# A recurrence, a mixture of experts and a squared-relu MLP on one core: token numbers copied to a tile of their own, the MLP in two passes over halves of its inner dimension, half of the weight conversions moved under the first pass

## The chip, the cores and the metric

The kernel runs on one core of a Trainium2 chip. The metric is device time in microseconds (us) of that core, as the median of several runs. The core's engines are TensorE (PE in the profile, its weight loads PEld), VectorE (DVE), ScalarE (ACT), GpSimd (POOL) and SyncE (SP), which here issues most of the DMAs. Each engine works through its own instructions in order and waits for others by semaphores.

## The reference

Three layers follow each other. All inputs are drawn at random; the MLP's weights `w_in` and `w_out` reach the kernel as float64 words.

```python
# 1. recurrence: batch 4, heads 8, seq 768, head_dim 48
for t in range(S):
    cur = np.einsum('bhd,bhe->bhde', u[None] * kt, vt)
    y[:, :, t] = np.einsum('bhd,bhde->bhe', rt, state + cur)
    state = wt[:, :, :, None] * state + np.einsum('bhd,bhe->bhde', kt, vt)
# 2. x: 3072 tokens x 384; 8 experts of width 1024, each token goes to one
e_idx = np.argmax(x @ w_gate, axis=1)
...
for e in range(E):
    h = np.maximum(x[mask] @ w1[e], 0.0)
    out[mask] = gate_w[mask, None] * eom[mask, e, None] * (h @ w2[e])
# 3. MLP: 384 -> 2048 -> 384
r = np.maximum(x @ w_in, 0.0)
out = (r * r) @ w_out
```

## The kernel before

The work runs in three stages. The recurrence (and the routing of its tokens) takes the first 285 us and is not touched.

**Experts.** The tokens of each expert form a block; blocks 1 to 7 hold room for 480, 440, 416, 404, 396, 388 and 384 tokens (`CAPS`). A block's rows are gathered from DRAM by POOL (`gather`, four indirect DMAs into `xg`, of which there is one buffer), scaled by their gate on ACT (`scale`), transposed on PE (`prep_x`, three per block) and split into a high and a low float32r part. Every product is made of three matmuls of such parts (`three`). The inner dimension of 1024 is walked in `KF` = 8 steps: `up(f)` is nine matmuls into `ph`, `down(f)` nine into the accumulators `po`. The weights arrive by SP's DMAs in halves (`load`) and are split three steps ahead: the high parts on ACT, the low part `w1l` on POOL, `w2l` on DVE. While block e is multiplied, block e+1 is loaded (f = 1 and 5), gathered (f = 2), scaled (f = 4) and transposed (f = 5, 6, 7). `put_ids`, issued by SP at f = 7, writes the numbers of the block's tokens from the last column of `xg` to DRAM (`x2_ids`, one 4-byte value to a row); `put` writes its results to `x2_cols`, one column to a token.

**Conversions.** Under blocks 1 to 7 the MLP's weights are turned from float64 to float32 on DVE: 32 pieces of 128x384, each in two steps, `convert_1` (three DVE instructions) and `convert_2` (three on DVE and a sum on POOL), loaded to `cq` and stored as `wi_f` and `wo_f`. `convert_step` does one step at a time, nine or ten per block.

**MLP.** The 3072 tokens form `NG` = 6 groups of 512. For each group the `KF2` = 16 steps of the inner dimension follow each other: `up2` is nine matmuls of 512 columns into `ph`, then relu on ACT (`rl`), square on DVE (`gg`), high part on ACT (`gh`), low part on DVE (`gl`); `down2` is twelve matmuls of 384 columns into four accumulators, three called `po` (one buffer each) and one `px`. PE's order is up2(n), down2(n-1), up2(n+1). After a group's last step the accumulators are copied to `ob`, by ACT and DVE in turn, and POOL writes them to the output by an indirect DMA.

The order on PE, DVE, ACT and SP is that of the code (`tc.manual_schedule`); POOL is in the scheduler's own order.

Of the kernel before, what the change touches and what calls it, by code (L numbers as in the profile page):

```python
# [21 lines left out]
def rwkv_moe_kernel(  # L22
# [64 lines left out]
    # of each expert: tokens, where its rows of each batch are, and from which of its tokens on  # L87
# [6 lines left out]
    # of each block  # L94
# [65 lines left out]
    def route_steps(b, xT, xr, wk, ps_t, ordered=False):  # L160
# [69 lines left out]
        if b == B - 2:  # L230
# [5 lines left out]
            # where its tiles' results go; a tile without a token goes past all  # L236
# [16 lines left out]
    def rows_of(gt, bv, K, nb):  # L253
        # where a block's rows come from; a slot past its tokens reads the row of zeros
# [12 lines left out]
    def finish_routing():  # L267
        # expert 0 first, the others by the number of their tokens
# [16 lines left out]
        # the first tokens of expert 0 have a block of their own  # L285
# [37 lines left out]
    with ExitStack() as actx:  # L323
# [230 lines left out]
    class Block:  # L554
        def __init__(self, P, cap, w1e, w2e, gcol):
# [3 lines left out]
            # where accumulators and transposes go  # L559
# [18 lines left out]
        def scale(self, eng=None):  # L578
            # the gate is not negative, so that it may come before the relu
# [61 lines left out]
        def put_ids(self, at):  # L641
            i, n = divmod(self.cap, 128)
            if i:
                nc.sync.dma_start(x2_ids[ds(at, i * 128)].rearrange("(i p) o -> p (i o)", p=128), self.xg[:, :i, DM + 1])
            if n:
                nc.sync.dma_start(x2_ids[i * 128:][ds(at, n)], self.xg[:n, i, DM + 1:DM + 2])
# [4 lines left out]
        # few tokens: they stand still, the weights stream  # L651
# [31 lines left out]
        def again(self, upto):  # L683
            # a block's first steps anew, into the same tiles; the sums begun there are closed first
# [10 lines left out]
        def whole(self, at):  # L695
# [3 lines left out]
            self.gather()  # L699
            self.put_ids(at)  # L700
            self.scale()
# [465 lines left out]
```

## Time and profile before

| | us |
|---|---|
| median of the runs | 979.07 |
| runs | 978.92, 979.07, 2810.91 |
| span of the profiled execution | 978.1 |

No own time is listed for the profiled execution beside its span. The span goes from its first to its last instruction and lies 0.97 us under the median of the runs.

| engine | busy us | share of the span |
|---|---|---|
| PE | 893.6 | 91% |
| PEld | 767.4 | 78% |
| DVE | 556.0 | 57% |
| ACT | 356.7 | 36% |
| POOL | 343.0 | 35% |

The shares are means over three stages with different limits; in the page's 40 slices PE falls to 6 to 8 tenths between slice 13 and slice 23 and is full after that, while DVE is at 6 to 9 tenths in the same slices and at 3 behind them. A stage is read from its own windows and waits.

### The profile page before, as it was taken

The page shows a single profiled execution, that of the slowest core. Times are in us where ns is not written, and L with a number is a line of the kernel's source. Part 1 is how long each engine was busy: PE and PEld are TensorE (multiplying, and loading weights), DVE is VectorE, ACT ScalarE, POOL GpSimd, SP SyncE. Part 2 cuts the span into 40 slices and gives each one's busy share as a digit, 9 for nine tenths or more (in the row PEclk, how much of TensorE's full clock was granted, in tenths as well). Part 3 has the DMA queues.
Part 4 walks back from the last instruction along what each step waited for, and adds up shares of the span by engine and source line. Part 5 has one row for each costly group of instructions (what it writes and reads, how often), then busy time and mean ns, then how long its engine had stood idle before and what let it go on. Part 6 is the DMA issues. An engine that isn't in the chain of part 4 may idle for free.

```text
span 978.1 us, 14225 instructions
## 1 busy us (share of the span) xinstructions
PE 893.6 (91%) x5324; PEld 767.4 (78%) x5324; DVE 556.0 (57%) x959; ACT 356.7 (36%) x721; POOL 343.0 (35%) x339
## 2 busy tenths in 40 slices
PE   4999999999786669898798899999999999999995
PEld 3667676777675559787698899999989999889995
DVE  6678887666824658677799733333333333333332
ACT  4235544233223234343344445432323323323221
POOL 9436564523411534435544744310201201101101
PEclk8589999999789799897999999999999999999998
DMA  9735463401134657757568634200200200000000
GB/s 197 206 75 111 97 147 74 110 2 64 48 107 110 210 125 232 193 168 245 186 189 231 187 91 129 82 33 1 65 1 0 65 1 1 33 1 1 33 1 33
DMA packets 152657, 94.99 MB, mean 97 GB/s; under 512 B 111996, under 2 KB 138540, under 8 KB 152580
## 3 DMA queue, kind: packets, MB, share of 16 engines
q1 hardware_dynamic: 146692, 79.12, 30.7%
q0 software_dynamic: 4912, 14.65, 4.3%
q8 instruction: 44, 0.72, 0.3%
q10 hardware_dynamic: 976, 0.22, 0.1%
q14 instruction: 33, 0.27, 0.1%
HBM read 73.05 MB, written 20.92 MB: 96 GB/s over the span
## 4 chain that ended last, share of the span: by engine, by line
issue 27%; PE 20%; DMA 9%; DVE 8%; POOL 5%; ACT 1%; SPq 1%; POOLq 0%; DVEq 0%; ACTq 0%
DMA x_ids<-xg 6%; PE ph L542 3%; PE ph L540 3%; PE ph L541 3%; PE po L541 3%; PE po L542 3%; PE po L540 3%; DVE cbf L923 2%; POOL out_dram L982 2%; DMA wo_f<-caf 1%; POOL xg L575 1%; DVE w2l L535 1%; DVE cq L921 1%; DVE hl L532 1%; DVE caf L920 1%
## 5 line engine op out<-in xcount | busy, mean ns | idle before, releaser
L966 DVE SCALAR_TENSOR_TENSOR gg<-ph,rl 128x512 f32<-128x512 f32 x96 | 66.4, 692 | 190.7 <-ACT rl L964 190.7
L964 ACT ACTIVATE rl<-ph 128x512 f32<-128x512 f32 x96 | 57.5, 599 | 186.4 <-PE ph L542 186.3
L535 DVE TENSOR_TENSOR gl<-gg,gh 128x512 fp32r<-128x512 f32 x96 | 66.7, 695 | 65.9 <-PE px L542 49.4
L531 ACT ACTIVATE hh<-ph 128x320 fp32r<-128x320 f32 (+7 forms) x64 | 32.5, 508 | 184.2 <-PE ph L542 180.5
L534 ACT CAST gh<-gg 128x512 fp32r<-128x512 f32 x96 | 59.5, 620 | 72.7 <-DVE gg L966 72.7
L535 POOL TENSOR_TENSOR w1l<-w1r,w1h 128x384 fp32r<-128x384 f32 x56 | 60.6, 1087 | 62.4 <-ACT w1h L534 62.3
L541 PE MATMUL po<-hl,w2h 128*128 128x320 f32 (+7 forms) x192 | 69.8, 364 | 11.8 <-DVE hl L532 11.7
L540 PE MATMUL po<-hh,w2h 128*128 128x320 f32 (+7 forms) x192 | 70.1, 372 | 1.9 <-DVE yT L637 1.9
L542 PE MATMUL po<-hh,w2l 128*128 128x320 f32 (+7 forms) x192 | 68.3, 356 | 0.0
L535 DVE TENSOR_TENSOR w2l<-w2r,w2h 128x384 fp32r<-128x384 f32 x64 | 54.4, 857 | 8.9 <-ACT w2h L534 8.3
L982 POOL DMA_INDIRECT out_dram<-ob,tokc x24 | 24.9, 1038 | 98.1 <-ACT ob L980 92.6
L535 POOL TENSOR_TENSOR x20l<-x2r,x20h 128x512 fp32r<-128x512 f32 x6 | 7.8, 1293 | 146.9 <-ACT x20h L534 146.9
L542 PE MATMUL ph<-x0h,w1l 128*128 128x320 f32 (+7 forms) x64 | 24.7, 386 | 32.8 <-POOL w1l L535 32.8
L532 DVE SCALAR_TENSOR_TENSOR hl<-ph,hh 128x320 fp32r<-128x320 f32 (+7 forms) x64 | 36.6, 572 | 26.8 <-ACT hh L531 26.7
L575 POOL DMA_INDIRECT xg<-x_rows,gi x28 | 27.3, 974 | 69.8 <-DMA x_ids<-xg 45.5
L541 PEld LDWEIGHTS po<-hl,w2h 128*128 128x128 f32 x192 | 37.9, 197 | 17.5 <-DVE hl L532 16.4
L456 PE MATMUL pa<-rA,kT 64*128 64x128 f32 x384 | 48.2, 316 | 2.3 <-DVE A L458 2.3
L477 PE MATMUL py<-A,vN 128*64 128x128 f32 x384 | 48.4, 310 | 0.0
L481 PE MATMUL py<-rA,St 64*64 64x128 f32 x320 | 47.8, 330 | 0.0
L456 PEld LDWEIGHTS pa<-rA,kT 64*128 64x128 f32 x384 | 37.4, 206 | 11.6 <-issue 6.5
L924 POOL TENSOR_TENSOR caf<-caf,cbf 128x384 f32<-128x384 f32 x32 | 33.3, 1041 | 33.0 <-DVE cbf L923 33.0
L438 POOL TENSOR_SCALAR_AFFINE_SELECT A<-g 128x1536 f32<-128x1536 f32 x16 | 30.7, 1921 | 38.4 <-DVE g L436 20.2
(796 smaller groups left out, 2564.4 us busy)
## 6 DMA issues: line engine op xcount, KB each, us to landing
w1r<-in_moe_w_dram SPq DMA_DIRECT2D x16, 768.0 KB, 5.4
w2r<-in_moe_w_dram SPq DMA_DIRECT2D x16, 768.0 KB, 6.9
cq<-in_moe_w_in_dram SPq DMA_DIRECT2D x16, 384.0 KB, 5.2
cq<-in_moe_w_out_dram SPq DMA_DIRECT2D x16, 384.0 KB, 5.6
wD<-in_w_dram SPq DMA_DIRECT2D x32, 144.0 KB, 3.0
kN<-in_k_dram SPq DMA_DIRECT2D x32, 144.0 KB, 3.0
rN<-in_r_dram SPq DMA_DIRECT2D x32, 144.0 KB, 3.1
vN<-in_v_dram SPq DMA_DIRECT2D x32, 144.0 KB, 2.7
```

The source lines that it names most:

```text
L456: nc.tensor.matmul(pa[j][:, ci], kT[pp, hf * HC + ci], rAb[pp, hf * HC + ci], start=True, stop=True)
L477: nc.tensor.matmul(py[64 * j:64 * j + 64, ci], vN[:, c, j], A[:, c, j], start=True, stop=c == 0)
L481: nc.tensor.matmul(py[pp, ci], St[pp, :, c], rAb[pp, c], start=False, stop=True)
L532: nc.vector.scalar_tensor_tensor(lo, src, 0.0, hi.bitcast(F32), op0=ALU.max, op1=ALU.subtract)
L534: nc.scalar.copy(hi, src)
L535: lo_eng.tensor_tensor(lo, src, hi.bitcast(F32), op=ALU.subtract)
L540: nc.tensor.matmul(out_, a_of(ah), b_of(bh), start=start, stop=False)
L541: nc.tensor.matmul(out_, a_of(ah), b_of(bl), start=False, stop=False)
L542: nc.tensor.matmul(out_, a_of(al), b_of(bh), start=False, stop=stop)
L964: nc.scalar.activation(rl, ph, AF.Relu)
L966: nc.vector.scalar_tensor_tensor(gg, ph, 0.0, rl, op0=ALU.max, op1=ALU.mult)
L982: ins = nc.gpsimd.indirect_dma_start(out=out[:, :], out_offset=IndirectOffsetOnAxis(ap=tokc[:, n:n + 1], axis=0), in_=ob, in_offset=None)
```

## The change

Three things are changed together; some comment lines go as well.

First, `scale` copies the token numbers from `xg` to a tile `xid` (three buffers), and `put_ids` reads that copy. Block 0 has no `scale` and keeps its `xg`.

Second, the MLP runs in two passes. The first takes steps f = 0 to 7 of all six groups and stores each group's sums to a DRAM tile `part`; the second takes f = 8 to 15, loads the parts and adds them on DVE as the sums leave PSUM. The tokens are loaded and split in both passes; `ob` has three buffers where it had six, and the next group is loaded at the first step of a group (it was the eighth of sixteen) and split at its steps 2, 4 and 6 (they were 10, 12 and 14).

Third, only the pieces of f = 0 to 7 are converted under the experts, in five steps per block. The other 16 pieces are loaded and converted in steps 8 to 39 of the MLP's first pass, one `convert_1` or `convert_2` to a step, and split straight from the converted tile without the way through DRAM.

```diff
         def scale(self, eng=None):
+            if self.ids is None:
+                self.ids = self.P.xb.tile([128, NTL], F32, name="xid", bufs=3)
+            i, n = divmod(self.cap, 128)
+            for ids, num in ([(self.ids[:, :i], self.xg[:, :i, DM + 1])] if i else []) + \
+                            ([(self.ids[:n, i:i + 1], self.xg[:n, i, DM + 1:DM + 2])] if n else []):
+                if eng:
+                    eng.tensor_copy(ids, num)
+                else:
+                    nc.scalar.copy(ids, num)
...
         def put_ids(self, at):
             i, n = divmod(self.cap, 128)
+            ids = self.xg[:, :, DM + 1] if self.ids is None else self.ids
             if i:
-                nc.sync.dma_start(x2_ids[ds(at, i * 128)].rearrange("(i p) o -> p (i o)", p=128), self.xg[:, :i, DM + 1])
+                nc.sync.dma_start(x2_ids[ds(at, i * 128)].rearrange("(i p) o -> p (i o)", p=128), ids[:, :i])
...
+    FH = KF2 // 2
+    part = [dram.tile([128, DM], F32, name=f"part{n}") for n in range(NT // 128)]
...
+    def split_converted(n):
+        f, which = divmod(n, 2)
+        (wi, wo)[which][f] = split([wp.tile([128, DM], F32R, name=f"w{'io'[which]}{f}{q}") for q in "hl"], converted.pop(n), nc.gpsimd)
...
+    def load_part(s):
+        for i in range(NI):
+            n = (s - NG) * NI + i
+            parts[n] = pbp.tile([128, DM], F32, name="pp")
+            nc.sync.dma_start(parts[n], part[n])
...
-            if f == KF2 - 1:
+            if l == FH - 1:
                 ob = obp.tile([128, DM], F32, name="ob")
-                if i % 2:
-                    nc.vector.tensor_copy(ob, pos[g][i][:, :DM])
-                else:
-                    nc.scalar.copy(ob, pos[g][i][:, :DM])
-                n = g * NI + i
+                n = s % NG * NI + i
+                if fs == 0:
+                    if i % 2:
+                        nc.vector.tensor_copy(ob, pos[s][i][:, :DM])
+                    else:
+                        nc.scalar.copy(ob, pos[s][i][:, :DM])
+                    nc.sync.dma_start(part[n], ob)
+                    continue
+                nc.vector.tensor_tensor(ob, pos[s][i][:, :DM], parts.pop(n), op=ALU.add)
...
-    NCV = 2 * KF2
-    steps2 = [(g, f) for g in range(NG) for f in range(KF2)]
+    NCV = 2 * FH
+    steps2 = [(s, f) for s in range(2 * NG) for f in range(s // NG * FH, s // NG * FH + FH)]
...
-            convert_step()
-            if f in (2, 7):
+            if f % 2 == 0 or f == KF - 1:
                 convert_step()
...
-        for n, (g, f) in enumerate(steps2):
+        late = [(fn, n) for n in range(NCV, 2 * KF2) for fn in (convert_1, convert_2)]
+        convert_load(NCV)
+        convert_load(NCV + 1)
+        for n, (s, f) in enumerate(steps2):
+            l = f % FH
             if n > 1:
-                up2(gb, g, f)
+                up2(gb, s, f)
...
-            if f == 7 and g + 1 < NG:
-                load_x(g + 1)
-            if g + 1 < NG and f in (10, 12, 14):
-                prep_x2(xb3 if g % 2 == 0 else xb2, g + 1, f // 2 - 5)
+            if l == 0 and s + 1 < 2 * NG:
+                load_x(s + 1)
+            if s >= NG and l == 3:
+                load_part(s)
+            if s + 1 < 2 * NG and l in (2, 4, 6):
+                prep_x2(xb3 if s % 2 == 0 else xb2, s + 1, l // 2 - 1)
+            if s and late:
+                fn, m = late.pop(0)
+                fn(m)
+                if fn is convert_1:
+                    if m + 2 < 2 * KF2:
+                        convert_load(m + 2)
+                    if m > NCV:
+                        split_converted(m - 1)
+                elif not late:
+                    split_converted(m)
             if n and n < len(steps2) - 2:
                 down2(*steps2[n - 1])
```

On POOL, under block 1, this stood before: the splits of block 1's first three steps, then the gather of block 2 (four indirect DMAs), then splits again, and `caf`, the sum that ends a conversion.

```order
L535 TENSOR_TENSOR w1l<-w1r,w1h 128x3x128 x3
L575 DMA xg<-x_rows,gi 128x386 x3
L575 DMA xg<-x_rows,gi 56x386
L535 TENSOR_TENSOR w1l<-w1r,w1h 128x3x128 x2
L924 TENSOR_TENSOR caf<-caf,cbf 128x384
```

And this stands there now:

```order
L535 TENSOR_TENSOR w1l<-w1r,w1h 128x3x128 x2
L576 DMA xg<-x_rows,gi 128x386 x3
L576 DMA xg<-x_rows,gi 56x386
L535 TENSOR_TENSOR w1l<-w1r,w1h 128x3x128 x4
L938 TENSOR_TENSOR caf<-caf,cbf 128x384
```

The gather has moved ahead of one more split, that of step f = 2; in each later block too it stands right behind the splits of the next block's steps 0 and 1.

On DVE, this stood before where one group of the MLP gives way to the next (the last step's square and low part, then the first step's, then the two copies to `ob`, then the next step's):

```order
L966 SCALAR_TENSOR_TENSOR gg<-ph,rl 128x512
L535 TENSOR_TENSOR gl<-gg,gh 128x512
L978 COPY ob<-po_7877 128x384
L978 COPY ob<-px 128x384
L966 SCALAR_TENSOR_TENSOR gg<-ph,rl 128x512
L535 TENSOR_TENSOR gl<-gg,gh 128x512
```

And this stands there now, in the first pass, from group 1 to group 2:

```order
L934 SCALAR_TENSOR_TENSOR caf<-cq,ca 128x384
L935 TENSOR_SCALAR cq<-caf 128x384
L937 SCALAR_TENSOR_TENSOR cbf<-cq 128x384
L992 SCALAR_TENSOR_TENSOR gg<-ph,rl 128x512
L535 TENSOR_TENSOR gl<-gg,gh 128x512
L925 TENSOR_SCALAR ca<-cq 128x384
L926 SCALAR_TENSOR_TENSOR ca<-cq,ca 128x384
L927 TENSOR_SCALAR cq<-cq 128x384
L1007 COPY ob<-po_7407 128x384
L1007 COPY ob<-px 128x384
L992 SCALAR_TENSOR_TENSOR gg<-ph,rl 128x512
L535 TENSOR_TENSOR gl<-gg,gh 128x512
```

Between every `gl` and the next `gg` there are now three instructions of a conversion, and at the change of group they stand ahead of the copies that free `po`.

## Rows read from the trace of the kernel before

**Rows 1.** Windows: stretch, length, busy us of PE, PEld, DVE, ACT, POOL; clock, DMA share, GB/s.
```profile
299.80:564.30 264.50, 217.94 (x1073) 199.11 (x1072) 197.00 (x328) 102.43 (x226) 121.77 (x118) 0.92 0.63 183
564.30:968.20 403.90, 403.90 (x2027) 364.70 (x2025) 144.44 (x209) 141.24 (x247) 70.50 (x64) 1.00 0.11 33
```
**Rows 2.** Waits from 285 to 568 us: total us, times, longest us.
```profile
POOL xg L575 <- DMA x_ids<-xg: 45.5, 4, 19.4
PE ph L542 <- POOL w1l L535: 32.8, 5, 15.1
PE po L541 <- DVE hl L532: 11.7, 10, 2.1
```
**Rows 3.** Timeline of PE in block 1: start us, length us; steps 4 and 5, transposes.
```profile
331.81 0.38 PE L540 MATMUL ph<-x0h,w1h 128*128 128x480 f32 x1
335.74 0.38 PE L540 MATMUL ph<-x0h,w1h 128*128 128x480 f32 x1
...
347.04 0.69 PE L596 MATMUL px<-ident,xg 128*128 128x128 f32 x4
```
**Rows 4.** Timeline of POOL in block 1: first gather for block 2, split after it.
```profile
319.83 0.97 POOL L575 DMA_INDIRECT xg<-x_rows,gi  x1 [19.38 <-DMA x_ids<-xg]
...
324.59 1.97 POOL L535 TENSOR_TENSOR w1l<-w1r,w1h 128x384 fp32r<-128x384 f32 x2
```
**Rows 5.** Timeline of SP in block 1: DMA issues.
```profile
306.17 0.40 SPq L644 DMA_DIRECT2D x_ids<-xg  x1
...
313.56 0.36 SPq L646 DMA_DIRECT2D x_ids<-xg  x1
...
322.91 0.38 SPq L649 DMA_DIRECT2D x_cols<-yT  x1
```
**Rows 6.** DMA issues: count, KB each, median us from issue to landing.
```profile
w2r<-in_moe_w_dram SPq DMA_DIRECT2D x16, 768.0 KB, 6.9
...
x2r<-x_cols SPq DMA_DIRECT2D x6, 768.0 KB, 4.6
...
x_ids<-xg SPq DMA_DIRECT2D x7, 1.5 KB, 10.2
...
out_dram<-ob,tokc POOLq DMA_INDIRECT x24, 2.6
```
**Rows 7.** Timeline of DVE and PE at the end of the MLP's second group.
```profile
696.58 0.69 DVE L966 SCALAR_TENSOR_TENSOR gg<-ph,rl 128x512 f32<-128x512 f32 x1 [2.12 <-ACT rl L964]
697.96 0.69 DVE L535 TENSOR_TENSOR gl<-gg,gh 128x512 fp32r<-128x512 f32 x1 [0.69 <-ACT gh L534]
700.78 0.69 DVE L966 SCALAR_TENSOR_TENSOR gg<-ph,rl 128x512 f32<-128x512 f32 x1 [2.14 <-ACT rl L964]
...
700.24 0.35 PE L542 MATMUL po<-wo15h,gl 128*128 128x384 f32 x1
...
704.63 0.34 PE L540 MATMUL po<-wo0h,gh 128*128 128x384 f32 x1
```
**Rows 8.** Timeline of DVE: a convert_1 and a convert_2, each with the instruction after it.
```profile
495.96 0.35 DVE L911 TENSOR_SCALAR ca<-cq 128x384 int32<-128x384 int32 x1
...
497.21 0.56 DVE L532 SCALAR_TENSOR_TENSOR hl<-ph,hh 128x396 fp32r<-128x396 f32 x1
...
498.63 0.55 DVE L920 SCALAR_TENSOR_TENSOR caf<-cq,ca 128x384 f32<-128x384 int32 x1
...
500.16 0.56 DVE L532 SCALAR_TENSOR_TENSOR hl<-ph,hh 128x396 fp32r<-128x396 f32 x1
```
**Rows 9.** Timeline of DVE and POOL: conversions beside POOL's work; a split of tokens.
```profile
409.02 1.16 DVE L911 TENSOR_SCALAR ca<-cq 128x384 int32<-128x384 int32 x1
...
510.68 4.47 DVE L921 TENSOR_SCALAR cq<-caf 128x384 int32<-128x384 int32 x1
...
512.97 1.96 POOL L535 TENSOR_TENSOR w1l<-w1r,w1h 128x384 fp32r<-128x384 f32 x2
...
694.33 1.30 POOL L535 TENSOR_TENSOR x22l<-x2r,x22h 128x512 fp32r<-128x512 f32 x1 [7.08 <-ACT x22h L534]
```

More of the change, by code (lines that the diff above doesn't have):

```diff
@@ L558, in __init__ @@
             self.upto = NT + 1
+            self.ids = None
             self.ps_y, self.y_names = ps_o, [f"po{d}" for d in range(KD)]
@@ L699, in whole @@
             self.gather()
+            self.scale()
             self.put_ids(at)
-            self.scale()
             for c in range(KD):
@@ L760, in put_ids_A @@
             n = blkA.rows(i)
-            ins = nc.sync.dma_start(x2_ids[ds(column(offA, i) if i else 0, n)], blkA.xg[:n, i, DM + 1:DM + 2])
+            ins = nc.sync.dma_start(x2_ids[ds(column(offA, i) if i else 0, n)], blkA.ids[:n, i:i + 1])
             for o in own:
@@ L942, in prep_w2, with load_x @@
         wo[f] = split([pool.tile([128, DM], F32R, name=f"wo{f}{q}") for q in "hl"], b_, nc.gpsimd)
[L944 to L951 removed]
+    def split_converted(n):
+        f, which = divmod(n, 2)
+        (wi, wo)[which][f] = split([wp.tile([128, DM], F32R, name=f"w{'io'[which]}{f}{q}") for q in "hl"], converted.pop(n), nc.gpsimd)
+    def load_x(s):
+        g = s % NG
+        rows[s] = rows_p.tile([128, KD, GT], F32, name="x2r")
+        nc.sync.dma_start(rows[s], x2_cols[:, :, g * GT:(g + 1) * GT].rearrange("c p t -> p c t"))
+        if s < NG:
+            idt = rows_p.tile([128, NI], F32, name="idt")
+            nc.sync.dma_start(idt, x2_ids[g * GT:(g + 1) * GT].rearrange("(i p) o -> p (i o)", p=128))
+            ids[g] = idt
+    def load_part(s):
[3 more added lines that the diff above has]
+            nc.sync.dma_start(parts[n], part[n])
+    xs, gs, pos, parts = {}, {}, {}, {}
     stores = []
     def prep_x2(pool, g, c):
[L955 removed]
+        if c == 0 and g < NG:
             nc.vector.tensor_copy(tokc[:, g * NI:(g + 1) * NI], ids[g])
@@ L967, in up2, with down2 @@
         gs[g, f] = split([gb.tile([128, GT], F32R, name="g" + q) for q in "hl"], gg, nc.vector)
-    def down2(g, f, last=False):
-        if f == 0:
-            pos[g] = [(ps_o if i < KD else ps_x).tile([128, 512], F32, name=f"po{i}" if i < KD else "px") for i in range(NI)]
+    def down2(s, f, last=False):
+        fs, l = divmod(f, FH)
+        if l == 0:
+            pos[s] = [(ps_o if i < KD else ps_x).tile([128, 512], F32, name=f"po{i}" if i < KD else "px") for i in range(NI)]
         for i in range(NI):
             for q in (f - 1, f) if last else (f,):
-                three(pos[g][i][:, :DM], gs[g, q], wo[q], lambda t: t[:, i * 128:(i + 1) * 128], lambda t: t, q == 0, q == KF2 - 1)
-            if f == KF2 - 1:
+                three(pos[s][i][:, :DM], gs[s, q], wo[q], lambda t: t[:, i * 128:(i + 1) * 128], lambda t: t, q % FH == 0, q % FH == FH - 1)
+            if l == FH - 1:
                 ob = obp.tile([128, DM], F32, name="ob")
-                if i % 2:
-                    nc.vector.tensor_copy(ob, pos[g][i][:, :DM])
-                else:
-                    nc.scalar.copy(ob, pos[g][i][:, :DM])
-                n = g * NI + i
+                n = s % NG * NI + i
[7 more added lines that the diff above has]
+                nc.vector.tensor_tensor(ob, pos[s][i][:, :DM], parts.pop(n), op=ALU.add)
                 ins = nc.gpsimd.indirect_dma_start(out=out[:, :], out_offset=IndirectOffsetOnAxis(ap=tokc[:, n:n + 1], axis=0),
```

24 lines of the change are left out of this document (7 added, 17 removed).

## The prediction

> **What bounds the kernel now.** I read the windows first, by stage. From 564.3 to 968.2 us PE is busy for all of 403.90 us at the full clock (1.00, 2.4 GHz): the MLP is bound by PE, and DVE with 144.44 us of work there is far from it. From 299.8 to 564.3 us, under blocks 1 to 7, PE is busy for 217.94 of 264.50 us at a mean clock of 0.92 [rows 1]. So the experts' stage has time to give and the MLP has none; the change must be judged by what it frees in the first and charges to the second.
>
> Next come the waits of that stage. PE waited 32.8 us, in five stalls, for `w1l`, the low part of a weight that POOL makes. POOL itself stood 45.5 us before the gather, waiting for DMA `x_ids<-xg`: the token numbers are still being written out of `xg`, and the gather must not overwrite it. PE waited a further 11.7 us for `hl`, which DVE makes [rows 2]. POOL's timeline shows why the first two are one stall: the gather begins after 19.38 us of waiting, and the `w1l` that PE needs is queued behind its four issues, 4.76 us later (324.59 - 319.83) [rows 4]. After such stalls the clock falls to its lower level for some us, which is the 0.92.
>
> What the stage would take without waits: a step of block 1 at full clock takes 335.74 - 331.81 = 3.93 us for 480 columns, and a step with transposes 0.69 us more [rows 3]. Steps scale with the columns: the seven blocks have 2908, so 8 x 3.93 x 2908/480 = 190.5 us, and with 6 x 3 transposes of 0.69 us, 12.4 us, some 203 us. The stage takes 264.5 us, so 61 us is there to be won at most.
>
> **The change: token numbers.** The copies cost ACT two instructions of at most four columns per block; they ride on `scale` and are hidden by ACT's idle time (102.43 us busy of 264.50 [rows 1]). The put then reads `xid`, so the gather waits only for the last transposes of the block before. Does it come in time? It now stands in front of the split of step 2. Between the last transposes and that split's use PE has five half steps (down 6, up 0, down 7, up 1, down 0), each half of 3.93 us at 480 columns and about 1.65 us at 400: 8.2 us. POOL needs 4.76 us for the gathers and about 1 us for the split (1.97 us for two [rows 4]). It fits with some 2 us to spare, so I let all of the 32.8 us go, and the slow clock behind it.
>
> What is late next is SP's queue, in block 1. Writes to `x2_ids` still wait for each other: the second put of block 1 left at 313.56, when the first, issued at 306.17, had landed; a put of block 0's results follows at 322.91, and only then can the weights of block 2 be asked for [rows 5]. The copy changes none of this. With 6.9 us to landing [rows 6] they arrive at about 330.3 us, while step 5 of block 1, in which ACT splits them, is then reached at 299.8 + 5 x 3.93 - 1.97 (step 0 has no down) = 317.5 us. ACT blocks there, and behind it stands the relu of step 6, which PE needs after step 6, up 7 and two sets of transposes, at 317.5 + 2 x 4.62 + 1.97 + 0.69 = 329.4 us. The split, the relu and `hl` come some 2 us after the landing, at 332.3: 3 us of stall, 1.5 us more as the next step's tokens are split behind it, and 1.5 us for the clock after it, 6 us in all (bounds 0 and 12). In the blocks after that a put of numbers holds SP for a median of 10.2 us [rows 6], but begins some six steps (20 us) before ACT needs the next load, which takes 6.9 us, so that nothing is late.
>
> **The change: half of the conversions.** A `convert_1` takes DVE 497.21 - 495.96 = 1.25 us, a `convert_2` 500.16 - 498.63 = 1.53 us [rows 8]. Of 32 pairs 16 leave the stage: 16 x 2.78 = 44 us of DVE's 197.00 us [rows 1]. DVE then has 153 us of work in a stage of some 215 us, where it had 197 in what would be 203 without waits: with the gathers alone freed, DVE would have become the bound. I leave 1 us per block for the waits that remain (the 11.7 us were 1.7 per block [rows 2]), 6 us for blocks 2 to 7. The stage: 203 + 6 + 6 = 215 us, that is 49.5 us less.
>
> **The change: the first pass.** A step is 700.78 - 696.58 = 4.20 us, and DVE is idle 2.14 us of it between `gl` and the next `gg`. `gl` ends at 698.65 and PE first needs it at 700.24, so DVE may fall 1.6 us behind before PE stalls [rows 7]. Both kinds of conversion step fit into 2.14 us, with 0.89 and 0.61 us left, if nothing disturbs them. But POOL now works at the same moment: the split of the converted weight (about 1 us) and, at steps 2, 4 and 6 of a group, the split of the next tokens (1.30 us [rows 9]), both released by ACT just when `gl` ends. Under the experts a DVE instruction that met POOL took 1.16 us where it takes 0.35 alone, and once 4.47 us, through POOL instructions in a row [rows 9]. So the wait in a pair of steps lies between 0.8 and 4.1 us; I take 2.3 us, both splits of POOL, since they stand back to back as in the longer row. The pair then runs 2.3 - 1.5 = 0.8 us over; three such pairs in a group use up the 1.6 us and cost PE about 0.5 us. At a change of group the conversion stands ahead of the copy that frees `po`: the second tile is needed at 704.63 [rows 7], the copy would be done then without any lag, and with the lag and one wait for POOL PE stalls about 1.8 us. Over the changes into groups 1 to 5 and the steps between: 0.9 + 3 x 2.3 + 2.7 = 10.5 us.
>
> The Trainium skill, page "SBUF — State Buffer", section "Who interferes with whom", says that DVE and GpSimd share one pair of ports, held for one whole instruction by whoever came first. The 1.16 us agrees with that, the 4.47 us does not, since several of POOL's instructions passed in it; by the rule as it stands the wait is one instruction each time, which is the second rival below.
>
> **The change: what else the two passes add.** PE's matmuls are the same 96 steps, so 403.90 us stays. Twelve groups where there were six: the extra splits are counted above for the first pass and stand beside idle engines in the second. The tokens of group 1 are asked for right after the last block's results are put, must wait for that landing, and take 4.6 us themselves [rows 6]; they are due two steps, 8.4 us, after: I charge 1 us, bounds 0 and 4. In the second pass DVE adds all four tiles, and the fourth waits for the first's output DMA, 2.6 us [rows 6], as only three `ob` are left; DVE's slack of 1.6 us covers most of it, at most 0.4 us at each of five changes. I take 0, as no conversion runs there. If that cover were gone, 2 us. The part stores and loads lie beside a DMA share of 0.11 [rows 1].
>
> **Sum.** -49.5 + 10.5 + 1 = -38 us on the span of 978.1, which is 940; the runs' median lies 1 us above the span, so 941 us.
>
> **The rivals.** *Only one instruction is waited for.* DVE waits 0.8 us in each step, 1.6 us per pair against 1.5 us left: nothing accumulates, and only the changes of group cost, some 1.5 us together. Then 979 - 49.5 + 1.5 + 1 = 932 us. For it speaks the 1.16 us row, against it that POOL's two splits come back to back. *The experts' stage is not freed in full.* The stall is there, but weights and gathers in the other blocks come as late as in block 1, since SP still stands behind each put of numbers: 4 us more in six blocks, 24 us, gives 965 us. Against it speaks the room of six steps. *The first pass starves DVE.* If the wait of a conversion step were that of the worst row, 4.47 - 0.36 = 4.1 us, in all of the 32 steps: 131 us, less the 16 x 1.5 us that are left, is 107 us, so 979 - 49.5 + 107 = 1036 us, slower than before. It decides from the point where a step waits 2.3 us on average (32 x 2.3 - 24 = 49.5); the mean of my pairs is half of that, and 4.47 us was seen once.
>
> **How the numbers follow.** Forecast 0.62, one instruction 0.18, stage not freed in full 0.14, starved 0.06. The range takes in the forecast with its bounds and the first rival less 6 us for smaller rests under the experts, and reaches to just short of the second: 926 to 962. Faster by over 2%, about what a measurement of this kernel can tell from no change, is below 959.5 us: the first two and most of a milder third, 0.90. Within 2%: 0.07. Slower: 0.03, from starvation.
>
> **What would show it.** In the profile of the changed kernel POOL no longer waits for `x_ids` before `xg`, and PE no longer for `w1l`; from the first `up` of block 1 to the MLP's first there are about 215 us, with one stall of some us late in block 1 behind ACT; the MLP's groups 1 to 4 take about 2 us longer than 33.5 us each and the second pass none. Wrong would be: a gather that waits for something else, DVE instructions of several us in the first pass, or ACT waiting for weights in every block.

## The result and the profile after

The changed kernel takes 943.65 us (median of 4 runs, 941.8 to 956.78), the kernel before 983.55 us (median of 4 runs beside it, among them the 2810.91 us): a ratio of 0.965, 95% interval 0.96 to 0.97. The profiled execution took 945.15 us with a span of 943.4. The ratio goes by the fast runs alone, so 956.78 and 2810.91 us are not in it. The forecast was 941 us, with 926 to 962 as its range.

The windows of the changed kernel, with the columns of [rows 1]: ahead of block 1, experts' stage, first pass, second pass.

```profile
0.00:292.40 292.40, 265.07 (x2228) 199.32 (x2229) 213.24 (x426) 112.60 (x248) 149.68 (x158) 0.94 0.47 112
292.40:509.90 217.50, 205.70 (x1073) 193.35 (x1072) 152.05 (x232) 102.81 (x237) 104.22 (x101) 0.98 0.74 179
509.90:718.00 208.10, 202.90 (x1007) 180.76 (x1007) 134.59 (x207) 83.14 (x152) 68.39 (x61) 1.00 0.26 85
718.00:933.40 215.40, 207.29 (x1021) 184.09 (x1019) 78.58 (x122) 66.67 (x114) 40.77 (x37) 0.99 0.18 60
```

Against [rows 1] the experts' stage is 47.0 us shorter and PE's mean clock in it rose from 0.92 to 0.98: of the 47.0 us, 34.8 are idle time of PE that went (46.6 before, 11.8 now), and 12.2 are PE's own busy time (217.94 before, 205.70 now), as the same matmuls ran at the higher mean clock. The MLP is 19.6 us longer (208.1 + 215.4 against 403.9). The windows of its first 48 steps and of the other 48 in the kernel before are these:

```profile
564.37:764.77 200.40, 200.40 (x1006) 180.91 (x1006) 71.59 (x103) 76.17 (x137) 48.11 (x44) 1.00 0.17 50
764.77:968.20 203.43, 203.43 (x1022) 183.72 (x1020) 72.85 (x106) 65.07 (x111) 22.32 (x20) 1.00 0.05 16
```

So the first pass is 7.7 and the second 12.0 us over. The stretch ahead of block 1, to which the change adds only a few small copies, is 7.4 us shorter. It took 291.6 to 310.3 us in the profiled executions of all kernels here, so these 7.4 us are taken as scatter between executions: the experiments are therefore read by the length of their stages first and by the whole time second.

The waits of the changed kernel in the experts' stage, columns as in [rows 2]:

```profile
POOL xg L576 <- PE px L607: 7.0, 3, 2.5
...
PE po L540 <- ACT hh L531: 5.4, 1, 5.4
PE po L540 <- DVE yT L648: 5.2, 3, 2.8
DVE ca L925 <- DMA cq<-in_moe_w_out_dram: 4.0, 1, 4.0
...
PE po L541 <- DVE hl L532: 1.2, 1, 1.2
```

POOL's 45.5 us before the gather [rows 2] have become 7.0 us, now for the transposes; PE's 32.8 us for `w1l` are gone, and its 11.7 us for `hl` are 1.2. What is left in one piece is the 5.4 us. Its story stands in the timeline of the changed kernel in block 1: SP's issues, then ACT, then PE (start us, length us; in brackets the idle time ahead and what ended it):

```profile
299.98 0.40 SPq L656 DMA_DIRECT2D x_ids<-xid  x1
307.57 0.36 SPq L658 DMA_DIRECT2D x_ids<-xid  x1
...
317.76 0.38 SPq L661 DMA_DIRECT2D x_cols<-yT  x1
318.35 0.40 SPq L307 DMA_DIRECT2D w1r<-in_moe_w_dram  x1
...
324.69 0.51 ACT L534 CAST w1h<-w1r 128x384 fp32r<-128x384 f32 x1 [11.11 <-DMA w1r<-in_moe_w_dram]
328.06 0.51 ACT L534 CAST w2h<-w2r 128x384 fp32r<-128x384 f32 x1 [2.86 <-DMA w2r<-in_moe_w_dram]
328.48 0.56 ACT L531 ACTIVATE hh<-ph 128x480 fp32r<-128x480 f32 x1
...
329.10 0.77 PE L540 MATMUL po<-hh,w2h 128*128 128x480 f32 x1 [5.39 <-ACT hh L531]
```

The second put of token numbers still leaves 7.6 us behind the first, for which it waits (as in [rows 5]). The put of block 0's results follows at 317.76, after SP stood 6.4 us for an earlier put to `x_cols`, and only then are the weights of block 2 asked for. ACT stands blocked on them, and the relu that PE needs is behind it on ACT.

The timeline of the changed kernel in the first pass: DVE and POOL in one step, then PE at the next change of group:

```profile
636.11 1.47 DVE L925 TENSOR_SCALAR ca<-cq 128x384 int32<-128x384 int32 x1
637.61 1.26 DVE L926 SCALAR_TENSOR_TENSOR ca<-cq,ca 128x384 int32<-128x384 int32 x1
...
636.06 1.29 POOL L535 TENSOR_TENSOR x21l<-x2r,x21h 128x512 fp32r<-128x512 f32 x1 [0.76 <-ACT x21h L534]
637.32 1.13 POOL L535 TENSOR_TENSOR wo12l<-caf,wo12h 128x384 fp32r<-128x384 f32 x1
...
655.92 0.44 PE L540 MATMUL po<-wo0h,gh 128*128 128x384 f32 x1 [1.27 <-DVE ob L1007]
```

The same two lines of `convert_1` in groups by form over groups 1 to 5 (count | busy us, mean ns | idle us), and the cast of the next group's token numbers:

```profile
L926 DVE SCALAR_TENSOR_TENSOR ca<-cq,ca 128x384 int32<-128x384 int32 x16 | 17.3, 1081 | 0.5
L925 DVE TENSOR_SCALAR ca<-cq 128x384 int32<-128x384 int32 x16 | 17.0, 1064 | 0.0
L982 DVE CAST tokc<-idt 128x4 int32<-128x4 f32 x4 | 5.1, 1274 | 0.0
```

The first of the two DVE instructions takes 0.35 us alone [rows 8], the other 0.56 (at 619.36 us, with POOL at rest). At 636 us the first ends just behind POOL's first split; the second begins in the gap and ends behind POOL's second. The cast took 0.17 us in group 0, where it began just ahead of POOL's split, and 1.27 us here, behind it. PE does not notice within a group. It stalls at the changes into groups 2, 3 and 4, by 1.3 to 1.4 us, where the copy of the accumulators stands behind the late conversion on DVE, and into group 5, by 1.1 us, behind a late copy on ACT.

The timeline of the changed kernel in the second pass, at the change into its third group: DVE, POOL's first output DMA, PE:

```profile
791.67 1.48 DVE L1012 TENSOR_TENSOR ob<-po,pp 128x384 f32<-128x384 f32 x3
798.03 0.56 DVE L1012 TENSOR_TENSOR ob<-px,pp 128x384 f32<-128x384 f32 x1 [4.87 <-DMA out_dram<-ob,tokc]
798.50 0.68 DVE L992 SCALAR_TENSOR_TENSOR gg<-ph,rl 128x512 f32<-128x512 f32 x1
...
792.50 0.99 POOL L1013 DMA_INDIRECT out_dram<-ob,tokc  x1 [7.97 <-DVE ob L1012]
...
799.89 0.44 PE L540 MATMUL po<-wo9h,gh 128*128 128x384 f32 x1 [2.57 <-ACT gh L534]
```

The group of all its fourth adds, 718 to 934 us:

```profile
L1012 DVE TENSOR_TENSOR ob<-px,pp 128x384 f32<-128x384 f32 x6 | 3.3, 558 | 20.0 <-DMA out_dram<-ob,tokc 20.0
```

Three adds run at once, the fourth waits for the first tile's DMA, and the next `gg` stands behind it on DVE; PE then waits for `gh`. The six waits add up to 20.0 us, PE's five stalls at the changes inside the pass are 1.1 to 2.6 us, 7.5 us together. The rest of the 12 us stands behind the longest stall, where the granted clock fell to between 0.53 and 0.60 from 801.5 to 805.5 us (the third group took 38.2 us, its neighbours 35.3), and at the end of the last group, which took 38.0 us where it took 35.9.

### The profile page after: what moved, and what is told of

The parts are those of the page before. It is cut to its first block, busy times and chain, and to the rows that moved or that the text cites. A ratio compares the mean times of both kernels' runs of the same rounds, so it can differ in the third digit from the quotient of the medians.

```text
span 943.4 us, 14307 instructions
## 1 busy us (share of the span) xinstructions
PE 881.0 (93%) x5324; PEld 757.5 (80%) x5324; DVE 579.0 (61%) x987; ACT 365.2 (39%) x750; POOL 365.0 (39%) x357
## 4 chain that ended last, share of the span: by engine, by line
PE 37%; issue 13%; DVE 10%; DMA 5%; ACT 3%; POOL 3%; SPq 0%; POOLq 0%; DVEq 0%; ACTq 0%
PE ph L541 6%; PE ph L540 6%; PE ph L542 6%; PE po L540 6%; PE po L542 5%; PE po L541 5%; DVE gg L992 2%; DVE gl L535 2%; ACT gh L534 2%; DVE ca L926 2%; DVE ca L925 1%; POOL out_dram L1013 1%; DMA w2r<-in_moe_w_dram 1%; DMA cq<-in_moe_w_out_dram 1%; DMA out_dram<-ob,tokc 1%
## 5 line engine op out<-in xcount | busy, mean ns | idle before, releaser
L535 DVE TENSOR_TENSOR w2l<-w2r,w2h 128x384 fp32r<-128x384 f32 x64 | 66.2, 1041 | 30.9 <-ACT w2h L534 30.6
L541 PE MATMUL po<-hl,w2h 128*128 128x320 f32 (+7 forms) x192 | 67.9, 354 | 1.2 <-DVE hl L532 1.2
L456 PE MATMUL pa<-rA,kT 64*128 64x128 f32 x384 | 45.9, 303 | 2.8 <-DVE A L458 2.8
L540 PEld LDWEIGHTS po<-hh,w2h 128*128 128x128 f32 x192 | 36.8, 194 | 13.2 <-DVE yT L648 6.2
L481 PE MATMUL py<-rA,St 64*64 64x128 f32 x320 | 47.1, 327 | 0.0
L477 PE MATMUL py<-A,vN 128*64 128x128 f32 x384 | 47.1, 304 | 0.0
L456 PEld LDWEIGHTS pa<-rA,kT 64*128 64x128 f32 x384 | 35.4, 195 | 11.6 <-issue 6.2
L438 POOL TENSOR_SCALAR_AFFINE_SELECT A<-g 128x1536 f32<-128x1536 f32 x16 | 32.2, 2012 | 32.2 <-DVE g L436 11.8
L244 POOL DMA_INDIRECT x_rows<-xr,dsi x24 | 26.2, 1093 | 44.3 <-issue 32.2
L481 PEld LDWEIGHTS py<-rA,St 64*64 64x64 f32 x320 | 29.2, 194 | 15.1 <-issue 12.7
```

The costliest lines, as they stand in the source:

```text
L456: nc.tensor.matmul(pa[j][:, ci], kT[pp, hf * HC + ci], rAb[pp, hf * HC + ci], start=True, stop=True)
L477: nc.tensor.matmul(py[64 * j:64 * j + 64, ci], vN[:, c, j], A[:, c, j], start=True, stop=c == 0)
L481: nc.tensor.matmul(py[pp, ci], St[pp, :, c], rAb[pp, c], start=False, stop=True)
L535: lo_eng.tensor_tensor(lo, src, hi.bitcast(F32), op=ALU.subtract)
L540: nc.tensor.matmul(out_, a_of(ah), b_of(bh), start=start, stop=False)
L541: nc.tensor.matmul(out_, a_of(ah), b_of(bl), start=False, stop=False)
```

## The experiments

Stage lengths are read from PE's timeline: from block 1's first `up` to the MLP's first `up2` (264.6 before, 217.5 after), then the first and the last 48 steps of the MLP (200.4 and 203.4 before, 208.1 and 215.5 after). The kernel before had medians of 977 to 979 us beside these runs.

### What the second pass loses

`e1_in_place`: the part that was loaded is added to in place.

```diff
-                ob = obp.tile([128, DM], F32, name="ob")
                 n = s % NG * NI + i
+                ob = parts.pop(n) if fs else obp.tile([128, DM], F32, name="ob")
...
-                nc.vector.tensor_tensor(ob, pos[s][i][:, :DM], parts.pop(n), op=ALU.add)
+                nc.vector.tensor_tensor(ob, pos[s][i][:, :DM], ob, op=ALU.add)
```

> The changed kernel, but in the second pass each tile of first-pass results is added to in place and sent to the output from where it lies, so that no add waits for one of the three output tiles. Theory (the second pass is 12.6 us over its 201.5 because the fourth add of a group waits for the first output's DMA, 3.4 to 4.9 us each time): the DVE waits before the fourth adds are gone, the PE stalls of 1.1 to 2.6 us in the six groups with them, the second pass takes some 204 to 206 us, and the time falls by about 10 us, to some 933 us. Rival (the stalls come from four adds in series on DVE and from the loads of part results and tokens beside them): the second pass stays within 3 us of 215 and the time at 941 to 944 us.

Measured: 933.1 us (ratio 0.9546, 0.9491 to 0.96), as the theory had it (though its base is wrong: these 48 steps took 203.4 us before, not 201.5). Its window of the second pass:

```profile
727.70:930.90 203.20, 203.17 (x1021) 183.41 (x1020) 79.00 (x122) 67.23 (x114) 40.81 (x37) 1.00 0.19 64
```

The fourth adds of its first five groups, grouped by form:

```profile
L1012 DVE TENSOR_TENSOR pp<-px,pp 128x384 f32<-128x384 f32 x5 | 2.7, 547 | 0.0
```

No add waits for an output DMA, PE is busy for the whole pass, and the pass has the length of the last 48 steps before. Four adds in series cost nothing, and the loads of parts, which here leave later, cost nothing either: the second pass lost its 12 us to the wait for an output tile and what came behind it.

### What the first pass loses

`e2_conv_behind`: in the first pass's loop the block that takes a conversion step is moved behind `down2`, with its copies.

```diff
+            if n and n < len(steps2) - 2:
+                down2(*steps2[n - 1])
             if s and late:
                 fn, m = late.pop(0)
                 fn(m)
...
-            if n and n < len(steps2) - 2:
-                down2(*steps2[n - 1])
```

> The changed kernel, but in the first pass a conversion is put behind the down step instead of ahead of it, so that at a change of group the copies that free the accumulators stand ahead of the conversion on DVE. Theory (the first pass is 7 us over because a copy at each of four changes of group waits behind a conversion, 1.1 to 1.4 us of PE stall each): those stalls go, the first pass shrinks from 208 to some 203 us, the time by 4 to 6 us to about 938 us. Rival (the excess comes from lag that DVE builds up over the group in meeting GpSimd, wherever the conversion stands): the lag then falls on the next gelu product instead, stalls of about the same sum turn up elsewhere in the groups, and the time stays within 2 us of 943.

Measured: 945.68 us (ratio 0.9675, 0.962 to 0.9731), no gain. The long stalls into groups 2 to 4 are gone, but groups 2 to 5 take 35.0, 34.7, 34.7 and 35.6 us (35.1, 35.4, 35.1 and 35.2 after): the lag is spread over the steps, up to 0.6 us each. The change into group 5 still stalls PE, by 1.3 us behind ACT's copy. The rival held; the place of the conversion is not what costs.

`e10_no_low`: leaves out the low part of the 16 weights that are converted in the first pass; the high part is used in its place.

```diff
-        (wi, wo)[which][f] = split([... for q in "hl"], converted.pop(n), nc.gpsimd)
+        hi = wp.tile([128, DM], F32R, name=f"w{'io'[which]}{f}h")
+        nc.scalar.copy(hi, converted.pop(n))
+        (wi, wo)[which][f] = hi, hi
```

> The changed kernel with one part of the computation left out: of the weights that are converted in the first pass no low part is made, the high part is used twice, so that GpSimd has 16 instructions fewer there; matmuls and DVE's instructions stay the same. Theory (a conversion's first two instructions take 1.06 and 1.08 us instead of 0.35 and 0.56 because GpSimd's splits run at the same moment, and this lag is paid at the changes of group): these two shrink towards 0.7 and 0.7 us, the stalls of 1.1 to 1.4 us at the changes shrink below 0.5 us and the first pass from 208 to 203 to 205 us. Rival (the conversions' own 2.8 us a pair use up the room in the steps): the groups stay at 35.1 us and the first pass at 207 to 208 us.

Measured: first pass 202.2 us, groups 33.4 to 34.1 us (whole time 949.18 us, ratio 0.9714, 0.9644 to 0.9784, its stretch ahead of block 1 308.8 us in the profiled execution). Its window of the first pass:

```profile
525.40:727.60 202.20, 202.02 (x1006) 180.85 (x1005) 124.66 (x207) 83.12 (x152) 51.36 (x45) 1.00 0.27 87
```

The same two lines of `convert_1` in it:

```profile
L925 DVE TENSOR_SCALAR ca<-cq 128x384 int32<-128x384 int32 x16 | 12.3, 769 | 0.0
L926 DVE SCALAR_TENSOR_TENSOR ca<-cq,ca 128x384 int32<-128x384 int32 x16 | 10.9, 680 | 0.6
```

With the same DVE instructions and 16 fewer of POOL's, the two lines fall from 1.06 and 1.08 to 0.77 and 0.68 us and the excess goes. The conversions fit in the room of the steps; meeting POOL there is what they cost.

`e11_skip_change`: the first step of a group takes no conversion step.

```diff
-            if s and late:
+            if s and l and late:
```

> The changed kernel, but the first step of each group in the first pass, in which the finished accumulators are copied out, holds no conversion step; the 32 conversion steps then stand in seven steps of a group instead of eight and reach four steps into group 5. Theory (each step runs a little over its room, the lag adds up over a group and is paid at the change; placing the conversion behind the copies only spread it): a free step per group gives back some 2 us, more than the 1.3 to 1.5 us of lag, so the groups fall from 35.1 to 33.6 us and the first pass from 208 to 202 to 203 us, the time by about 5 us to 938 us. Rival (the excess is a fixed price of each conversion that nothing gives back): the first pass stays at 207 to 208 us.

Measured: 946.44 us (ratio 0.9704, 0.9638 to 0.977), first pass 206.5 us, so the 202 to 203 was missed. Groups 1 to 4 are as the theory had it: 33.5, 33.6, 33.6 and 34.2 us. Two other groups took it back. Group 0 was 35.2 us (33.6 after; 33.4 to 37.0 over the kernels with two passes): ACT waits 3.8 us there for the tokens of group 1 (and DVE 4.6 us for their numbers), which were asked for late behind the last block's results, and the next `rl` stands behind their split on ACT. Group 5 was 36.4 us, for this reason in ACT's timeline:

```profile
712.48 0.51 ACT L534 CAST wo15h<-caf 128x384 fp32r<-128x384 f32 x1 [3.96 <-POOL caf L938]
```

The last converted weight is split right behind its own `convert_2`, so ACT waits for POOL's sum with the next `rl` behind it, and PE stalls 1.9 us. In the changed kernel that split stands in the first step of group 5, ahead of ACT's copy, and is the stall of 1.1 us there.

### What each part is worth under the experts

`e3_ids_alone`: the first part of the change's diff put into the kernel before.

```diff
+                    nc.scalar.copy(ids, num)
...
-                nc.sync.dma_start(x2_ids[ds(at, i * 128)]..., self.xg[:, :i, DM + 1])
+                nc.sync.dma_start(x2_ids[ds(at, i * 128)]..., ids[:, :i])
```

> The kernel before with the copy of the token numbers alone: one pass of the MLP, all 32 conversions under the experts. My prediction's reading: with the gathers freed, DVE with 197 us of work becomes the bound of the experts' stage, which takes some 225 to 235 us instead of 217; the MLP keeps its 403.9 us, so the time is 944 to 954 us, no better than the full change. Rival (the gathers' wait was the whole loss, DVE's 197 us still fit in): the stage takes 217 to 221 us, and as the MLP pays nothing for two passes the time is 925 to 932 us, better than the full change.

Measured: 964.42 us (ratio 0.9858, 0.9793 to 0.9924), the stage 248.1 us. Neither number was right: DVE does become the engine that holds PE up, but the stage is longer than my 225 to 235 us. Its window of the stage:

```profile
310.30:558.40 248.10, 215.33 (x1073) 198.57 (x1072) 198.74 (x328) 103.32 (x237) 124.06 (x117) 0.94 0.74 196
```

Its waits there:

```profile
PE po L541 <- DVE hl L532: 27.5, 12, 10.3
...
DVE ca L921 <- DMA cq<-in_moe_w_out_dram: 11.9, 1, 11.9
```

Its timeline in block 1, SP and then DVE:

```profile
324.09 0.36 SPq L656 DMA_DIRECT2D x_ids<-xid  x1
...
325.12 0.42 SPq L914 DMA_DIRECT2D cq<-in_moe_w_out_dram  x1
...
333.40 0.36 DVE L921 TENSOR_SCALAR ca<-cq 128x384 int32<-128x384 int32 x1 [11.90 <-DMA cq<-in_moe_w_out_dram]
```

PE's wait has moved from `w1l` to `hl`. Once, in block 1, DVE stands 11.9 us for a conversion's load that was issued behind the second put of token numbers; in the other blocks `hl` is 0.4 to 3.0 us late, once or twice a block, behind conversions. That is not DVE's own work alone: it also waits there up to 2 us for the store of an earlier converted tile, once 3.1 us for POOL's sum, and some of its conversion instructions take 2.4 to 3.6 us, where alone they take 0.55.

`e8_ids_load`: `e3_ids_alone` and the edit of `e6_load_first`, below.

> The kernel before with the copy of the token numbers and with block 2's weights asked for ahead of the put of block 0's results; one pass of the MLP. If DVE bounds the experts' stage, the earlier weights give nothing over the copy alone (within 2 us of it). If it does not, the stall of block 1 goes as in the changed kernel, some 5 us less than the copy alone, 920 to 927 us by the rival of that run.

Measured: 961.94 us (ratio 0.9862, 0.9811 to 0.9912), as the copy alone; the stage 251.5 us. The earlier weights gave nothing: in block 1, 47.0 us where the copy alone has 44.0, DVE waits 14.4 us for the conversion's load.

`e9_one_pass_early`: `e8_ids_load`, and the second conversion's load issued ahead of the puts.

```diff
+        convert_load(1)
+        put_A(1)
         blocks[1].put_ids(column(off, 1))
-        put_A(1)
-        convert_load(1)
         put_A(2)
```

> The kernel before with the copy of the token numbers, one pass, all conversions under the experts; block 2's weights are asked for ahead of the put of block 0's results, and the second conversion's load ahead of block 1's puts of token numbers. The copy alone left an experts' stage of 248 us, in which DVE waited 11.9 us once for a conversion's load that stood behind those puts, and hl came 1.6 to 3.0 us late in each later block. Theory (one late load, the rest DVE's own 197 us of work): block 1 falls from 44 to some 34 us, blocks 2 to 7 stay at about 204 us, the stage takes 236 to 240 us and the time is about 950 us, still above the full change. Rival (late loads on SyncE's queue were the whole excess): the stage falls to 215 to 222 us and the time to 925 to 933 us.

Measured: 960.82 us (ratio 0.98, 0.9723 to 0.9876), the stage 246.0 us. Block 1 fell from 44.0 to 40.1 us only, as DVE then waited 8.2 us for a later load of `cq`, so the theory's 236 to 240 us were missed too; blocks 2 to 7 took 205.9 us (204.1 with the copy alone, 176.8 after). The rival, late loads as the whole excess, is out: 29 us of the difference to the changed kernel lie in blocks 2 to 7, where none is waited for, and go with the 16 pairs. How much of it is DVE's work and how much their waits (stores, up to 3.0 us; POOL's sum, up to 3.1 us; meeting POOL) was not separated. With one pass no median came below 960 us.

`e4_no_ids`: the changed kernel, and `put_ids` reads `xg` again.

> The changed kernel without the copy of the token numbers: the put reads them from the gathered tile again, while the MLP stays in two passes with half of the conversions in the first. Theory (the 47 us come from the gather's wait, not from the conversions): GpSimd waits some 40 us for the numbers' puts again, PE for the low parts of the weights, the experts' stage takes 250 to 260 us, and with the MLP's 20 us more the time is 975 to 990 us, no faster than before. Rival (most of the gain is DVE's 44 us of conversions that left): the stage falls to about 230 us and the time to 955 us.

Measured: 982.98 us (ratio 1.0113, 1.0053 to 1.0173), within the theory's 975 to 990, the stage 247.3 us where it had 250 to 260. Its waits in the stage:

```profile
POOL xg L576 <- DMA x_ids<-xg: 42.8, 4, 19.0
...
PE ph L542 <- POOL w1l L535: 35.3, 6, 14.7
```

The old pair of waits is back, 42.8 and 35.3 us against 45.5 and 32.8 [rows 2]. Still the stage gained 17.3 us from the conversions that left, and the MLP took 16.5 us of it back.

`e5_passes_ids`: the changed kernel with all conversions under the experts.

```diff
-    NCV = 2 * FH
+    NCV = 2 * KF2
...
-            if f % 2 == 0 or f == KF - 1:
+            convert_step()
+            if f in (2, 7):
                 convert_step()
```

> The changed kernel with the copy and both passes, but with all 32 conversions under the experts as before, so that the first pass holds none. Theory (conversions in the first pass cost most of its 7 us): the first pass takes 202 to 204 us, the second stays at 215, and the experts' stage has the length that the copy alone gives, 225 to 235 us by my reading that DVE bounds it: time 948 to 958 us. Rival (the first pass's excess is from the twelve groups themselves, stores of parts and splits): it stays at 207 to 208 us; and if DVE does not bound the experts' stage it takes 217 to 221 us, time 937 to 943 us.

Measured: 985.16 us (ratio 1.0092, 1.0057 to 1.0127), the stage 249.2, the passes 209.7 and 213.9 us: far above the 948 to 958 us expected, since the stage is as long as with the copy alone. The first pass's excess here is in group 1, 42.1 us: PE stalls 5.9 us, and the granted clock behind it is 0.60 from 600 to 605 us. DVE's copy of the fourth accumulator waited for a store of parts, which left late behind this kernel's weight loads:

```profile
600.62 0.56 DVE L1007 COPY ob<-px 128x384 f32<-128x384 f32 x1 [9.18 <-DMA part<-ob]
```

The other five groups took 33.4 to 33.6 us, so that with a group 1 like them the pass is some 201 us: stores and second splits cost under 1 us, and the conversions cost the changed kernel's first pass 6 to 7 us. Two passes without moving the conversions are no faster than before.

### The stall in block 1, and the edits together

`e6_load_first`: in step 1 of block 1.

```diff
                 blk0.turn_back()
-                blk0.put(column(off, 0))
...
                 nxt.load(f // 5)
+            if e == 1 and f == 1:
+                blk0.put(column(off, 0))
```

> The changed kernel, but in block 1 the load of block 2's weights is issued ahead of the put of block 0's results on SyncE's queue. Theory (the 5.4 us stall of PE at 329 us is ACT standing blocked on these weights, which SyncE asked for late): ACT's wait of 11 us for w1r shrinks below 5 us, the stall goes, block 1 shrinks from 40.7 to about 35 us and the time by some 5 us, to 938 to 939 us. Rival (ACT and POOL are late there for block 1's other work, so the stall only moves to the next step): block 1 shrinks by less than 2 us, time 942 to 944 us.

Measured: 939.75 us (ratio 0.9619, 0.9567 to 0.9672). Its window of block 1:

```profile
298.80:332.90 34.10, 32.42 (x152) 26.94 (x152) 17.69 (x28) 15.24 (x35) 11.47 (x11) 1.00 0.74 155
```

The rows of its timeline that answer to those above, ACT's and PE's:

```profile
327.33 0.52 ACT L534 CAST w1h<-w1r 128x384 fp32r<-128x384 f32 x1 [7.34 <-DMA w1r<-in_moe_w_dram]
...
330.36 0.48 PE L540 MATMUL po<-hh,w2h 128*128 128x480 f32 x1 [1.04 <-ACT hh L531]
```

ACT's wait fell from 11.1 to 7.3 us, not below 5, but that is enough: the stall is 1.04 us, block 1 34.1 us instead of 40.7 and the stage 212.9. The cause is shown; in the whole time the 4 us are too few to be told from the changed kernel's interval.

`e7_all`: the edits of `e1_in_place`, `e2_conv_behind` and `e6_load_first`.

> The three edits together: results added in place in the second pass, conversions behind the down step in the first, block 2's weights asked for ahead of the put of block 0's results. If the three stalls are separate and each goes, the gains add: 10, 5 and 5 us, and the time is about 923 us (918 to 928). If the rivals hold (four adds in series, lag wherever the conversion stands, stall only moved) it stays above 936 us.

Measured: 929.25 us (ratio 0.9488, 0.9428 to 0.9548): stage 210.8, passes 210.4 and 203.1 us. That is 1 us above the range in which the gains add: two of the three are there, but the first pass gave nothing back, as in `e2_conv_behind`, and its group 0 took 37.0 us.

`e12_best`: the edits of `e1_in_place`, `e6_load_first`, `e11_skip_change` and the early load of `e9_one_pass_early`.

> All edits that should each remove a wait of the changed kernel: results added in place in the second pass, no conversion in the first step of a group, block 2's weights asked for ahead of the put of block 0's results, the second conversion's load ahead of block 1's puts of token numbers. If they add up: experts' stage 211, first pass 203, second 203 us, time 919 to 923 us, some 5 us below the version with the conversions behind the down step (929 us median). If the first pass keeps its excess, 925 to 929 us.

Measured: 931.37 us (ratio 0.9524, 0.9448 to 0.96). Its windows of the stage and the two passes:

```profile
295.80:506.00 210.20, 203.62 (x1072) 191.62 (x1071) 151.60 (x232) 102.81 (x237) 103.83 (x100) 0.99 0.74 186
506.00:712.50 206.50, 204.36 (x1007) 182.02 (x1006) 137.06 (x207) 83.19 (x152) 68.36 (x61) 0.99 0.26 86
712.50:915.70 203.20, 203.18 (x1022) 183.43 (x1020) 78.99 (x122) 67.24 (x114) 40.83 (x37) 1.00 0.19 64
```

The first pass keeps its 206.5 us, as in `e11_skip_change`, and that was the expectation's second case, missed by some 2 us. Here all of the excess is in group 5, 38.0 us: the split of the last weight stalls PE 1.9 us as before, and the granted clock is 0.74 in the 4 us behind it. The intervals of `e1_in_place`, `e7_all` and `e12_best` overlap: the add in place is the part whose gain over the changed kernel is shown, about 10 us; the three medians lie 10.5 to 14.4 us below that of the changed kernel.

## Why the prediction was right, and where it was off

The time came within 3 us, and part of that is luck: one term of the sum was 12 us off, and a stretch ahead of block 1 that happened to be 7.4 us shorter made up for most of that. Without that scatter the forecast's -38 us stand against -27.3: -47.1, +7.7 and +12.1. On equal early stretches the sum would have missed by some 11 us, still inside the range.

**Token numbers.** Right. The gather is free of `x_ids`, the `w1l` stall is gone, and `e4_no_ids` brings both back. The room that I worked out held: no `w1l` came late in any block.

**SP's queue in block 1.** Right in place and chain, with ACT blocked on the weights behind the put. PE's stall is 5.39 us where I had 3, as ACT waits a second time, 2.86 us, for `w2r`; with what follows it I had 6 us, and block 1 fell by 6.6 us when the load went first. `e6_load_first` shows the cause.

**Half of the conversions.** Right that with the gathers alone freed DVE would hold PE up. I had given that case no size in the sum, and the one that I expected for it later, 225 to 235 us, was too small: it is 248, since the conversions also wait, for loads, stores and POOL. The two parts do not add up: the copy alone gives 16.5 us, the conversions alone 17.3, both 47.1. Either delay hides the other: with the conversions alone moved `w1l` still stalls PE in blocks 1 to 6, with the copy alone `hl` does in all seven, and with both PE waits 1.2 us for `hl` once; whichever is left still sets the pace. The stage at 217.5 against my 215 is 2.5 us off.

**The first pass.** The mechanism was right, the size too high: I took 2.3 us of waiting for POOL in each pair of steps and 10.5 us in all. The wait is (1.06 - 0.35) + (1.08 - 0.56) = 1.2 us a pair, all of it in `convert_1`, or 1.5 us with the cast of token numbers, which I had not counted and which meets POOL in the same steps (4 x 1.1 us over 16 pairs). With 0.6 us for the late tokens of group 1 (I had 1) the excess is 7.7 us, and groups 2 to 5 run 1.5 to 1.9 us over where I had about 2. That lag comes due at the change of group is as I said, but `e2_conv_behind` shows that it cannot be moved away, and `e10_no_low` that it is POOL's. The rival had the whole price at 1.5 us, with one instruction waited out in each step, 1.6 us a pair, which it took for no more than the 1.5 of room; but the pair at 636 us, which meets both splits, waits (1.47 - 0.35) + (1.26 - 0.56) = 1.8 us, both in its first step. That does add up, and so the rival came out too low. The Trainium skill's rule, page "SBUF — State Buffer", section "Who interferes with whom", is that whoever issues first gets the shared ports for a whole instruction; in this pass the trace agrees with it, since at 636 us DVE gets in between two POOL instructions.

**The second pass: the term that failed.** I took 0 us because the fourth add would wait "for the first's output DMA, 2.6 us [rows 6]", and DVE's slack of 1.6 us would cover most. The wait was there, but 3.4 to 4.9 us long at each of the five changes (0.9 at the end, 20.0 us in all), and cost 12.1 us; my case "if that cover were gone, 2 us" was too small as well. The 2.6 us were a landing under the MLP before, whose output DMAs ran alone. In the second pass the median is 3.4 and the longest 5.6 us, and at 792 us three of the four loads of parts leave together with the first output. That these loads stretch the landing was not tried by itself, but the same trace speaks for it: behind the last group, where no part is left to load, all four outputs land in 2.6 us again, while at the five changes the medians are 3.0 to 4.9 us. With the add in place, where a part can be loaded only when an output has left its tile, the median of all is 2.7 us.

**The other rivals.** The stage was freed in all blocks: blocks 2 to 7 take 25.3 to 32.8 us, 176.8 in all, with three stalls of 0.9 to 2.8 us for `yT`, the block's results on their way out. Nothing starved DVE in the first pass: its longest conversion instruction there took 1.48 us.

## What to carry to other kernels

Two waits that hold up the same engine in the same stretch hide each other: try each removal alone and both together before giving either a price, since here 16.5 and 17.3 us alone made 47.1 together. A landing time read where a queue runs alone is no price for a place where the change adds transfers; better still, take the wait away, here by adding into the tile that was loaded, so that no output tile is needed. And work put into an engine's idle time is charged by what it meets there, here POOL's splits: what counts is how often the two meet, and a lag that fits in each step still comes due where the steps change.

## What was not expected of the hardware

Nearly the same instructions ahead of block 1 took 291.6 to 310.3 us from one profiled execution to the next, with a mean granted clock of 0.94 (292.4 us, after), 0.90 (299.8 us, before) and 0.88 (310.3 us, the copy alone). Most of the difference is PE's own busy time: 265.07, 271.75 and 280.61 us. That is as much as most of the edits here are worth, and the kernels differ there only by a few small copies and, in two of them, by the order of a few DMA issues.

Under the experts a DVE instruction can still stay behind several of POOL's, as in [rows 9]. Here is one in the timeline of the changed kernel, DVE and then POOL:

```profile
427.45 4.73 DVE L535 TENSOR_TENSOR w2l<-w2r,w2h 128x384 fp32r<-128x384 f32 x1 [0.24 <-ACT w2h L534]
432.11 0.57 DVE L648 COPY yT<-po 128x404 f32<-128x404 f32 x1
...
427.87 1.03 POOL L535 TENSOR_TENSOR w1l<-w1r,w1h 128x384 fp32r<-128x384 f32 x1
428.85 1.03 POOL L938 TENSOR_TENSOR caf<-caf,cbf 128x384 f32<-128x384 f32 x1
429.82 1.94 POOL L535 TENSOR_TENSOR w1l<-w1r,w1h 128x384 fp32r<-128x384 f32 x2
```

It ends 0.4 us after the fourth of POOL's instructions (alone it takes 0.55 us), and the copy to `yT` behind it is the one that PE waits 2.8 us for. At 636 us DVE came in after one, though there too POOL's next one followed at once. What decides who goes next is open.
